# Order of rows and number of stores in the last token block of a fused retention + MLP kernel

## The chip, the cores and the metric

The kernel runs on one core of one Trainium2 chip. The metric is the device time of one execution in microseconds. Before the change it is 282.61 us, the median of 3 runs (282.43 to 282.74).

## The reference: what is computed

Inputs are q, k, v of shape (8 batches, 8 heads, 576 positions, 64) and two matrices, w_in (512 x 2048) and w_out (2048 x 512), all float32. The result is 4608 x 512, float32.

```python
scores = scale * np.matmul(q, k.transpose(0, 1, 3, 2))        # scale = 1/8
Dmat = np.where(rel >= 0, gamma[:, None, None] ** rel, 0.0)    # rel = i - j, one gamma for each head
attn = np.matmul(scores * Dmat, v)                             # retention: causal decay, no softmax
x = attn.transpose(0, 2, 1, 3).reshape(B * S, H * D)           # 4608 tokens x 512
h = x @ w_in
g = 0.5 * h * (1.0 + erf(h / sqrt(2)))                         # exact GELU
out = g @ w_out
```

## The kernel before

**Blocks and units.** The 4608 tokens are taken in 9 blocks (t = 0 to 8) of 512. A block is made of four units, ts = 0 to 3, each of them 128 token rows. Most units are 128 positions running of one batch. As 576 is 4 x 128 + 64, the ninth unit of each pair of batches is a short one: 64 positions of one batch and 64 of the next. `rows_of` (L1080) gives one range of output rows for an ordinary unit and two ranges of 64 rows for a short one. In the last block, t = 8, the units are 32 to 35 of 36, and ts = 3 is a short one.

**Second product.** For blocks 1 to 8, g times w_out is done with seven products of quarter size in place of eight (a Strassen scheme). The 512 tokens are split into an upper half (`half` 0: ts = 0, 1) and a lower one (`half` 1: ts = 2, 3), and the 512 output columns into two times 256. So there are four quadrants, named in the code c11 and c12 (upper half, left and right columns) and c21 and c22 (lower half). Within a half, r = 0 or 1 says which of its two units of 128 rows: a quadrant of one r is 128 rows x 256 columns, 128 KB. In the last block r = 0 stands for ts = 0 and 2, and r = 1 for ts = 1 and 3; so c21 and c22 of r = 1 are the short unit.

The products run in the order `SECOND = "1267534"` (L200), each of them for both r and in two parts of 8 matmuls. `fast` (L1146) issues the matmuls. What is done with the results stands in `add_second` (L1252): products 1 and 2 are copied from PSUM by ScalarE (product 2 of r gives c11, L1233); products 6, 7, 5, 3 and 4 are combined by ScalarE copies (L1243) and VectorE additions (L1238, L1247). The last VectorE addition for c22 hangs on product 5, that for c12 on product 3, that for c21 on product 4. In blocks 1 to 7 both r go through one chain (`rows_at_once`, L1141); in the last block each r has a chain of its own, with instructions of 128 x 256.

**Stores.** `store` (L1296) issues the DMAs on SyncE's queue, one for each range of rows that `rows_of` gives. In the last block there are, for each r, three store operations (L1358 to L1363): the whole lower half unit (512 columns) once c21 and c22 are there, c11 once it is there, and c12 once it is there. An ordinary unit is one DMA and a short one is two DMAs of 64 rows each. So the last block has seven DMAs: c11 of r = 0, c11 of r = 1, c12 of r = 0, c12 of r = 1, the lower unit of r = 0 (256 KB), and the lower unit of r = 1 (two of 64 x 512, 128 KB each). They are issued in this order.

**What sets the order.** A planner (class `Plan`, L30, and the loop at L1584) simulates the engines with assumed durations and gives out one operation after another: on each engine it takes, of those that can start within a small slack, the one with the lowest due time. The due times of the second product come from `W` (L324), which walks the `stream` of pieces in order (L311 to L315). SyncE works through its operations one after another, and waits at each for what the DMA reads. Besides, the DMAs use eight semaphores in turn, so that a DMA also waits until the eighth one before it has landed. After the last instruction SyncE waits at the end of the program for the DMAs of all eight (these waits carry L1654), and then all engines meet at a barrier.

Of the kernel before, what the change touches and what calls it, by code (L numbers as in the profile page):

```python
# [29 lines left out]
class Plan:  # L30
# [9 lines left out]
    def add(self, name, engine, dur, deps, fn, due=0.0, lag=0.12, **more):  # L40
        assert name not in self.ops, name
        op = self.ops[name] = Op(name, engine, dur, deps, fn, due, lag, **more)
        for d in op.deps:
            if d.startswith("land"):
                self.users.setdefault(d, []).append(op)
            dep = self.ops.get(d)
            if dep is None or dep.end is None:
                op.waits += 1
                self.later.setdefault(d, []).append(op)
            else:  # L50
                op.ready = max(op.ready, dep.end + dep.lag)
        if not op.waits:
            self.released(op)
        return op
# [53 lines left out]
def kernel(  # L108
# [23 lines left out]
    N_BLK = n_tok // TOK  # L132
# [28 lines left out]
    def slot_of(i):  # L161
        return pair_with(i)[0]

    v_order = [i for i in range(N_U) if i not in kept]
    n = v_order.index(pair_of[1, 1][0])
# [34 lines left out]
    SECOND = "1267534"  # L200
# [20 lines left out]
    add = P.add  # L221
# [81 lines left out]
    stream = []  # L303
    for t in range(N_BLK):
        if t < 2:
            cuts = CUTS if t == 0 else (0, 256, 512)
            for lo, hi in zip(cuts, cuts[1:]):
                stream.append([("1", t, m, 2, lo, hi) for m in K_ORDER[::2]])
        else:
            stream.append([one for block in LAYOUT[t] for one in laid(t, block)])  # L310
        if t < FAST:  # L311
            stream.append([("2", t, ts, m, m + 2) for m in range(0, N_DF, 2) for ts in range(2)])
            stream.append([("2", t, ts, m, m + 4) for ts in range(2, 4) for m in range(0, N_DF, 4)])
        else:
            stream.append([("2", t, p, r, n, part) for n, p in enumerate(SECOND) for r in range(2) for part in range(2)])  # L315

    def piece_time(one):
        if one[0] == "u":
# [6 lines left out]
    W = {}  # L325
# [6 lines left out]
    for one, at in W.items():  # L332
        key = ("1" if one[0] == "u" else one[0], one[1])
# [6 lines left out]
    for nm, src, eng, tag in (("q", q, nc.sync, "t"), ("k", k, nc.scalar, "t"), ("v", v, nc.sync, "o0")):  # L340
        t = first[nm] = (o_pool if nm == "v" else f_pool).tile([128, H, D], FP32, tag=tag, name=f"{nm}32")
# [214 lines left out]
    st = {i: {} for i in range(N_U)}  # L556
# [318 lines left out]
    for i in range(N_U):  # L875
        bp, ci, j = units[i]
        n = group_of[i]
# [28 lines left out]
        n, short = slot_of(i), i in tails  # L906
# [21 lines left out]
    for i in v_order:  # L928
        due = need[group_of[i]] + 3.0 if i not in kept else need[group_of[pair_of[1, 1][0]]] - 2.0
        n = v_order.index(i)  # L930
# [11 lines left out]
    for bp, ci in order_of_states:  # L942
# [16 lines left out]
        n = pair[0]  # L959
# [120 lines left out]
    def rows_of(t, ts):  # L1080
        bp, ci, j = units[t * 4 + ts]
        if j is not None:
            return [((2 * bp + j) * S + ci * C, 0, C)]
        return [((2 * bp + jj) * S + ci * C, TAIL * jj, TAIL) for jj in range(2)]
# [56 lines left out]
    def rows_at_once(t):  # L1141
        return [(0, 1)] if t < N_BLK - 1 else [(0,), (1,)]
# [153 lines left out]
    def store(t, half, cols=slice(None), rows=(0, 1), ends=True):  # L1296
        for r in rows:
            for row, p0, n in rows_of(t, 2 * half + r):
                nc.sync.dma_start(out[row:row + n, cols], fold["o", t, half][p0:p0 + n, r, cols])
        send("hw", T["sp"] + 1.0, STORE if ends and cols == slice(None) else STORE / 4)  # L1300
        if ends:
            o_ring[half].give(T["sp"] + 4.0)
# [12 lines left out]
    for run in stream:  # L1315
        for one in run:
            nm = f"mlp{one}"
            if one[0] == "1":
                _, t, m0, n, lo, hi = one
                xs = [f"x{i}" for i in range((t * TOK + lo) // C, (t * TOK + hi - 1) // C + 1)]  # L1320
                add(nm, "pe", piece_time(one), [f"land wi{m0 // 2}", *xs], lambda one=one: mlp1(one), W[one], DRAIN, banks=1)
                add(f"gelu{one}", "act", 0.08 + n * (hi - lo) * 0.00084, [nm, "warm_act"], lambda one=one: gelu(one), W[one] + 0.5,
                    at=lambda t=t, m0=m0: 0.0 if (t, m0 % 8 // 4) in g_tiles or not t else g_ring[m0 % 8 // 4].at())
            elif one[0] == "u":
                _, t, kp, p = one
                key = f"c{('u', t, kp)}"
                deps = [f"x{i}" for i in range(4 * t, 4 * t + 4)]
                deps += [f"ui{kp}.{LEFT[p]}"] if p in LEFT else []
                deps += [f"xs{t}.{RIGHT[p]}"] if p in RIGHT else []
                deps += [key + BEHIND[p]] if p in BEHIND else []  # L1330
                add(nm, "pe", piece_time(one), deps, lambda one=one: unit(one), W[one], DRAIN, banks=int(p in "321"))
                if p == PRODUCTS[-1]:
                    add_chain(("u", t, kp), 2, {q_: [f"mlp{('u', t, kp, q_)}"] for q_ in PRODUCTS},
                              {q_: W["u", t, kp, q_] for q_ in PRODUCTS})
            elif isinstance(one[2], str):
                _, t, p, r, n, part = one
                kps = (2 * part, 2 * part + 1)
                rs = next(x for x in rows_at_once(t) if r in x)
                key = f"c{('2', t, rs)}"
                deps = []  # L1340
                if p in G_SUM:
                    deps += [f"gs{t},{part}.{G_SUM[p]}"]
                else:
                    deps += gelus_of(t, kps, int(p != "1"))
                deps += [f"ws{kp}.{W_SUM[p]}" for kp in kps] if p in W_SUM else []
                deps += [f"land wo{kp + 4 * (p != '1')}" for kp in kps] if p in "123" else []
                deps += [key + BEHIND2[p] + (str(r) if p == "2" else "")] if p in BEHIND2 else []
                add(nm, "pe", piece_time(one), deps, lambda one=one: fast(one), W[one], DRAIN,
                    banks=int(not part and (p == "1" or p in OPENS and r == rs[0])))
                if p == SECOND[-1] and r == rs[-1] and part:  # L1350
                    at_ = {q_: {x: W["2", t, q_, x, SECOND.index(q_), 1] for x in rs} for q_ in SECOND}
                    add_second(("2", t, rs), len(rs), {q_: [f"mlp{('2', t, q_, x, SECOND.index(q_), 1)}" for x in rs] for q_ in SECOND},
                               {q_: max(at_[q_].values()) for q_ in SECOND})
                    if t < N_BLK - 1:
                        add(f"st{t},1", "sp", 1.1, [key + "c21", key + "c22"], lambda t=t: store(t, 1), W[one])
                        add(f"st{t},0", "sp", 1.1, [key + "c12"] + [key + f"c11{x}" for x in rs], lambda t=t: store(t, 0), W[one] + 1)
                    else:
                        add(f"st{t},1.{r}", "sp", 0.5, [key + "c21", key + "c22"],  # L1358
                            lambda t=t, r=r: store(t, 1, slice(None), (r,), ends=False), W[one])
                        add(f"st{t},0a.{r}", "sp", 0.5, [key + f"c11{r}"],  # L1360
                            lambda t=t, r=r: store(t, 0, slice(0, 256), (r,), ends=False), W[one])
                        add(f"st{t},0.{r}", "sp", 0.5, [key + "c12"],
                            lambda t=t, r=r: store(t, 0, slice(256, 512), (r,), ends=False), W[one] + 1)  # L1363
            else:
                _, t, ts, n0, n1 = one
                ms = K_ORDER[n0:n1]
                gl = [o for o in W if o[0] == "1" and o[1] == t and any(o[2] <= m < o[2] + o[3] for m in ms)
                      and o[4] < ts * 128 + 128 and o[5] > ts * 128]
                before = [f"mlp{('2', t, ts, 2 * n0 - n1, n0)}"] if n0 else []
                add(nm, "pe", piece_time(one), [f"land wo{m // 2}" for m in ms] + [f"gelu{o}" for o in gl] + before,  # L1370
                    lambda one=one: plain(one), W[one], DRAIN, banks=int(n0 == 0))
                if n1 == N_DF:
                    add(f"po{t},{ts}", "act", 0.5, [nm], lambda t=t, ts=ts: plain_out(t, ts), W[one] + 0.5,
                        at=lambda t=t, ts=ts: 0.0 if ("o", t, ts // 2) in fold else o_ring[ts // 2].at())
                    if ts % 2:
                        add(f"st{t},{ts // 2}", "sp", 1.1, [f"po{t},{ts - 1}", f"po{t},{ts}"], lambda t=t, ts=ts: store(t, ts // 2), W[one] + 1)
# [149 lines left out]
    for _ in range(N_WARM):  # L1526
        b, t = bank([128, 512], FP32, "warm")
# [131 lines left out]
```

## Time and profile before

| | us |
|---|---|
| median of 3 runs | 282.61 (282.43 to 282.74) |
| profiled execution: its time | 282.72 |
| profiled execution: span, first to last instruction | 280.7 |
| first matmul of the second product of the last block | 263.7 |
| last VectorE instruction (c21 of r = 1), start | 276.12 |
| last DMA issued by SyncE, start | 277.09 |

The granted TensorE clock is 1.000 over the whole span. The span is what the profile covers; the execution's own time is 2.0 us longer. An instruction row of the timeline gives start and length in us, the engine (SPq is SyncE's DMA queue, DVE is VectorE, PE is TensorE, ACT is ScalarE), the source line, what it writes and reads, and in brackets how long the engine had been idle before it and what ended that. For DMAs the instruction's length is only the issue; "to landing" is counted from the start of the issue to the completion of the transfer.

### The profile page before, as it was taken

The page shows a single profiled execution, that of the slowest core. Times are in us where ns is not written, and L with a number is a line of the kernel's source. Part 1 is how long each engine was busy: PE and PEld are TensorE (multiplying, and loading weights), DVE is VectorE, ACT ScalarE, POOL GpSimd, SP SyncE. Part 2 cuts the span into 40 slices and gives each one's busy share as a digit, 9 for nine tenths or more (in the row PEclk, how much of TensorE's full clock was granted, in tenths as well). Part 3 has the DMA queues.
Part 4 walks back from the last instruction along what each step waited for, and adds up shares of the span by engine and source line. Part 5 has one row for each costly group of instructions (what it writes and reads, how often), then busy time and mean ns, then how long its engine had stood idle before and what let it go on. Part 6 is the DMA issues. An engine that isn't in the chain of part 4 may idle for free.

```text
span 280.7 us, 8896 instructions
## 1 busy us (share of the span) xinstructions
PE 273.9 (98%) x3731; PEld 220.0 (78%) x3731; DVE 230.1 (82%) x438; ACT 174.0 (62%) x414; POOL 110.4 (39%) x139
## 2 busy tenths in 40 slices
PE   7999999999999999999999999999999999999993
PEld 2679767578888688868887888688868888888782
DVE  5870465699999998999799999987987799969832
ACT  7678733646438952995297319852898379528740
POOL 8967778847546086233326804705000000000000
PEclk9999999999999999999999999999999999999999
DMA  9999999999999999999989999999800040022013
GB/s 148 165 182 186 178 186 165 142 238 133 127 139 173 197 114 128 140 230 145 156 188 57 134 112 172 210 117 135 184 22 2 6 149 2 4 75 77 0 40 112
DMA packets 152071, 35.57 MB, mean 127 GB/s; under 512 B 141024, under 2 KB 147680, under 8 KB 152032
## 3 DMA queue, kind: packets, MB, share of 16 engines
q0 software_dynamic: 115792, 17.97, 98.1%
q1 hardware_dynamic: 35200, 16.78, 34.9%
q8 instruction: 29, 0.48, 0.8%
q10 hardware_dynamic: 1040, 0.26, 0.4%
q14 instruction: 10, 0.08, 0.1%
HBM read 36.70 MB, written 9.44 MB: 164 GB/s over the span
## 4 chain that ended last, share of the span: by engine, by line
PE 87%; DVE 4%; POOL 4%; DMA 3%; issue 1%; ACT 0%; POOLq 0%; DVEq 0%
PE oT L229 39%; PE hT L229 16%; PE zT L229 10%; PE yT L229 7%; PE o_ps L229 4%; DMA w_in<-in_moe_w_in_dram 3%; PE sc L229 2%; POOL qk_ld L517 2%; PE u_ps L229 2%; DVE s L999 1%; PE qk_ps L233 1%; DVE ret L652 1%; POOL v_ld L517 1%; POOL w_in L523 1%; DVE g L999 0%
## 5 line engine op out<-in xcount | busy, mean ns | idle before, releaser
L229 PEld LDWEIGHTS <-g 128*128 128x128 bf16 x576 | 55.1, 98 | 12.5 <-issue 0.2
L229 PEld LDWEIGHTS <-w_in 128*128 128x128 bf16 x656 | 53.0, 98 | 13.3 <-DMA w_in<-in_moe_w_in_dram 0.4
L229 PE MATMUL hT<-xT,w_in 128*128 128x128 bf16 (+2 forms) x480 | 53.5, 266 | 0.3 <-DMA w_in<-in_moe_w_in_dram 0.3
L229 PEld LDWEIGHTS <-wi_sum 128*128 128x128 bf16 x440 | 42.8, 98 | 6.6
L1099 ACT ACTIVATE g<-hT 128x512 bf16<-128x512 f32 (+1 forms) x72 | 35.9, 505 | 19.5 <-PE hT L229 17.7
L229 PE MATMUL oT<-w_out,g 128*128 128x256 bf16 (+1 forms) x320 | 45.6, 294 | 0.0
L517 POOL DMA_DIRECT2D qk_ld<-in_q_dram x31 | 28.0, 905 | 35.1 <-DMA qkT<-qk_ld 22.8
L229 PEld LDWEIGHTS <-s 128*128 128x128 bf16 x384 | 36.8, 98 | 5.6 <-DVE s L999 0.5
L517 POOL DMA_DIRECT2D v_ld<-in_v_dram x31 | 28.1, 910 | 22.8 <-ACT vh L824 9.5
L229 PE MATMUL oT<-w_sum,s 128*128 128x256 bf16 x256 | 32.4, 273 | 0.2 <-ACT o_sb L1243 0.2
L824 ACT ACTIVATE vh<-v_ld,dv 128x64 bf16<-128x64 bf16 x112 | 31.2, 346 | 1.0 <-DMA v_ld<-in_v_dram 1.0
L229 PE MATMUL oT<-w_sum,g 128*128 128x256 bf16 x256 | 30.8, 273 | 0.0
L517 POOL DMA_DIRECT2D qk_ld<-in_k_dram x31 | 28.0, 903 | 5.5 <-DMA v_ld<-in_v_dram 5.2
L1243 ACT COPY o_sb<-oT 128x512 f32<-128x512 f32 (+1 forms) x27 | 14.5, 538 | 25.2 <-PE oT L229 13.3
L1212 ACT ACTIVATE g<-zT 128x512 bf16<-128x512 f32 x44 | 25.9, 614 | 0.1
L652 DVE TENSOR_TENSOR ret<-sc,msk 128x512 bf16<-128x512 f32 x36 | 23.2, 687 | 1.4 <-PE sc L229 1.4
L1247 DVE TENSOR_TENSOR o_sb<-o_sb,oT 128x512 f32<-128x512 f32 (+1 forms) x27 | 16.8, 629 | 8.8 <-PE oT L229 4.5
L570 ACT COPY q<-yT 128x512 f32<-128x512 f32 x18 | 10.3, 594 | 21.8 <-PE yT L229 21.8
L855 DVE TENSOR_TENSOR xT<-o_ps,dqT 128x512 bf16<-128x512 f32 x26 | 16.8, 686 | 3.3 <-PE o_ps L229 3.3
L821 DVE TENSOR_TENSOR vh<-v_ld,dv 128x512 bf16<-128x512 bf16 x22 | 15.0, 688 | 3.4 <-DMA v_ld<-in_v_dram 3.4
L1221 DVE TENSOR_TENSOR zT<-q,zT 128x512 f32<-128x512 f32 x22 | 15.3, 695 | 1.0 <-PE zT L229 0.6
L1191 DVE TENSOR_TENSOR q<-q,zT 128x512 f32<-128x512 f32 x22 | 14.5, 684 | 1.7 <-PE zT L229 0.8
(170 smaller groups left out, 453.6 us busy)
## 6 DMA issues: line engine op xcount, KB each, us to landing
out_dram<-o_sb SPq DMA_DIRECT2D x30, 256.0 KB, 3.9
qk_ld<-in_q_dram POOLq DMA_DIRECT2D x31, 128.0 KB, 7.6
qk_ld<-in_k_dram POOLq DMA_DIRECT2D x31, 128.0 KB, 8.5
v_ld<-in_v_dram POOLq DMA_DIRECT2D x31, 128.0 KB, 8.0
w_in<-in_moe_w_in_dram POOLq DMA_DIRECT2D x8, 256.0 KB, 8.6
w_out<-in_moe_w_out_dram POOLq DMA_DIRECT2D x8, 256.0 KB, 7.8
out_dram<-o_sb SPq DMA_DIRECT2D x12, 128.0 KB, 2.7
v_ld<-in_v_dram POOLq DMA_DIRECT2D x8, 64.0 KB, 6.4
```

Source lines behind the costliest of these rows:

```text
L229: return nc.tensor.matmul(*args, **more)
L517: nc.gpsimd.dma_start(dst, src[2 * bp + j, :, ci * C:ci * C + C, :].rearrange("h s d -> s h d"))
L652: nc.vector.tensor_tensor(r, t, by, op=ALU.mult)
L821: nc.vector.tensor_tensor(vh, loaded[i][1], dv[:, :, ci:ci + 1].to_broadcast([128, H, D]), op=ALU.mult)
L824: nc.scalar.activation(vh[:, h], loaded[i][1][:, h], AF.Copy, scale=dv[:, h, ci:ci + 1])
L855: nc.vector.tensor_tensor(dst, o, dqT[:, :, ci * C:ci * C + C], op=ALU.mult)
L1099: nc.scalar.activation(g_of(t, m0)[:, m0 % 2:m0 % 2 + n, m0 // 8, lo:hi], hT, AF.Gelu)
L1191: nc.vector.tensor_tensor(q_, q_, chain[key]["Z"][1], op=ALU.subtract)
L1212: nc.scalar.activation(target(key, what), chain[key][n][1], AF.Gelu)
L1221: nc.vector.tensor_tensor(to, chain[key]["q"], z, op=ALU.add)
L1243: nc.scalar.copy(target(key, what), chain[key][n][1])
L1247: nc.vector.tensor_tensor(to, to, chain[key][n][1], op=ALU.add)
```

## The change

In the last block the two r change places: within each product r = 1 goes first, then r = 0. And the three store operations of each r become four, one for each quadrant: c11, c22, c12, c21, each waiting only for its own last instruction. Lower quadrants of r = 1 (the short unit) are two DMAs of 64 x 256 (64 KB each), all the others one of 128 x 256 (128 KB). That makes ten DMAs in place of seven, for the same 1 MB.

```diff
         else:
-            stream.append([("2", t, p, r, n, part) for n, p in enumerate(SECOND) for r in range(2) for part in range(2)])
+            stream.append([("2", t, p, r, n, part) for n, p in enumerate(SECOND) for r in ((0, 1), (1, 0))[t == N_BLK - 1]
+                           for part in range(2)])
...
                     else:
-                        add(f"st{t},1.{r}", "sp", 0.5, [key + "c21", key + "c22"],
-                            lambda t=t, r=r: store(t, 1, slice(None), (r,), ends=False), W[one])
-                        add(f"st{t},0a.{r}", "sp", 0.5, [key + f"c11{r}"],
-                            lambda t=t, r=r: store(t, 0, slice(0, 256), (r,), ends=False), W[one])
-                        add(f"st{t},0.{r}", "sp", 0.5, [key + "c12"],
-                            lambda t=t, r=r: store(t, 0, slice(256, 512), (r,), ends=False), W[one] + 1)
+                        for h, c, on in ((0, 0, f"c11{r}"), (1, 1, "c22"), (0, 1, "c12"), (1, 0, "c21")):
+                            add(f"st{t},{h}{c}.{r}", "sp", 0.4, [key + on],
+                                lambda t=t, r=r, h=h, c=c: store(t, h, slice(256 * c, 256 * c + 256), (r,), ends=False), W[one] + c)
```

## The prediction

> **What bounds the kernel now.** I read the page first, then the chain of waits, then the last 10 us of the timeline, engine by engine, then SyncE's stores one at a time and its waits at the end.
>
> ```profile
> span 280.7 us, 8896 instructions
> PE 273.9 (98%) x3731; PEld 220.0 (78%) x3731; DVE 230.1 (82%) x438; ACT 174.0 (62%) x414; POOL 110.4 (39%) x139
> ...
> PE 87%; DVE 4%; POOL 4%; DMA 3%; issue 1%; ACT 0%; POOLq 0%; DVEq 0%
> ```
>
> TensorE is busy for 98% of the span: nearly all of the time is matmuls. The change touches none, so what it can move is the stretch behind the last one. In the timeline of VectorE:
>
> ```profile
> 273.03 0.89 DVE L1247 TENSOR_TENSOR o_sb<-o_sb,oT 128x256 f32<-128x256 f32 x2 [0.45 <-ACT o_sb L1243]
> 274.37 0.42 DVE L1247 TENSOR_TENSOR o_sb<-o_sb,oT 128x256 f32<-128x256 f32 x1 [0.45 <-PE oT L229]
> 275.24 0.42 DVE L1247 TENSOR_TENSOR o_sb<-o_sb,oT 128x256 f32<-128x256 f32 x1 [0.45 <-PE oT L229]
> 276.12 0.42 DVE L1247 TENSOR_TENSOR o_sb<-o_sb,oT 128x256 f32<-128x256 f32 x1 [0.45 <-PE oT L229]
> ```
>
> Quadrants come out every 0.87 us, paced by TensorE (each row ends an idle time "<-PE"); the last, c21 of r = 1, is done at 276.12 + 0.42 = 276.54. From there to 280.7 there are 4.1 us with no engine computing. SyncE's DMAs one at a time (start in us behind the durations in ns; below each, its time to landing): c12 of r = 1, the 256 KB store of the lower unit of r = 0, and the two stores of the short unit:
>
> ```profile
> L1299 SPq DMA_DIRECT2D out_dram<-o_sb x1: 333/333/333, 274.8 to 274.8; - x1
> DMA to landing us min/median/max: 1.7/1.7/1.7
> ...
> L1299 SPq DMA_DIRECT2D out_dram<-o_sb x1: 332/332/332, 275.7 to 275.7; - x1
> DMA to landing us min/median/max: 2.0/2.0/2.0
> ...
> L1299 SPq DMA_DIRECT2D out_dram<-o_sb x1: 472/472/472, 276.6 to 276.6; - x1
> DMA to landing us min/median/max: 2.3/2.3/2.3
> ...
> L1299 SPq DMA_DIRECT2D out_dram<-o_sb x1: 587/587/587, 277.1 to 277.1; - x1
> DMA to landing us min/median/max: 2.4/2.4/2.4
> ```
>
> The timeline gives these starts as 274.82, 275.69, 276.56 and 277.09. SyncE stands ready each time: a store starts 0.02 to 0.03 us after its VectorE instruction ends. Only the fourth waits for the queue, for 0.53 us behind the third. It lands at 277.09 + 2.4 = 279.47 or so (two decimals from the wait that it ends, next). SyncE's waits at the end of the program:
>
> ```profile
> L1654 SPq EVENT_SEMAPHORE  x6: 28/28/28, 279.5 to 279.8; - x6
> ...
> L1654 SPq DRAIN  x3: 7/7/7, 279.9 to 280.2; - x3
> ```
>
> The first of six comes free at 279.48 (the last store has landed); five more follow at 0.06 us each, then the barrier, 0.8 us. So the end is: last VectorE instruction, 0.55 us until the last issue, 2.4 us to landing, 1.2 us of closing.
>
> **The change part by part.** The sum is made against this execution: span 280.67, time 282.72; the median of 282.61 lies 0.1 below, and I subtract from the median.
>
> *TensorE, VectorE, ScalarE, GpSimd: 0.* The change swaps which 128 rows go first. The built order of the changed kernel has the same instructions of the same shapes with the same waits on these four; only addresses differ. So quadrants still come out at 272.57 (c22), 273.45, 273.92 (c12), 274.79, 275.66 (c21) and 276.54, of r = 1 and r = 0 in turn. Both r of one product read the same g and wait for the same GELUs, so the swap makes neither wait longer. If that cover were gone, a matmul group late by one quadrant would cost 0.87.
>
> *SyncE: three DMAs more.* Its new order, from the built program: c11 of r = 1, of r = 0; c22 of r = 1 (two), of r = 0; c12 of r = 1, of r = 0; c21 of r = 1 (two), of r = 0. No DMA is held by the eight semaphores: the last reuses that of c11 of r = 0, issued some 9 us before.
>
> First, is SyncE late when the last quadrants come? A pair of 64-row stores took 0.472 + 0.587 plus gaps of 0.05 = 1.16; a 128-row store 0.33 alone and up to 0.58 straight behind such a pair (the store at 226.75). With the dearer figures: c22 pair 272.60 to 273.76, c22 of r = 0 to 274.39, c12 of r = 1 to at most 275.02, c12 of r = 0 to at most 275.65, just before 275.66. With 0.38 per 128-row store the queue has caught up by 274.8. So the c21 pair starts at 275.69 either way.
>
> Next, the last store. The c21 pair holds SyncE for 1.16 (until 276.85) if 64 x 256 issues like 64 x 512, or for 0.77 (276.46, no wait) if like 128 x 256. Half the bytes should press less on the second issue; the form with 64 rows is the nearer row. I take 276.80, between 276.57 and 276.87. Before: 277.09. Gain 0.29.
>
> Landing: a 128 x 256 store takes 1.7 with nothing close ahead of it (c12, twice). Of a 128-row store behind a 64-row pair there is one row with no loads about, the 256 KB store at 226.75: 2.4, against 2.0 for such a store at 275.69, 0.4 more. The new pair has half the bytes of that one. So 1.7 to 2.1; I take 1.8, nearer to the row of its own form. Landing at 278.60 in place of 279.47: gain 0.87 in all, issue included.
>
> Closing: the last DMA uses the sixth of the eight semaphores in place of the third, so two waits follow in place of five: 3 x 0.06 = 0.18. The other stores have landed by then. The barrier of 0.8 stays.
>
> Sum: 0.87 + 0.18 = 1.05. 282.61 - 1.05 = 281.6 us. With both unknowns at their good ends (276.57 + 1.7 = 278.27): gain 1.38, 281.2. At their bad ends (276.87 + 2.1 = 278.97): gain 0.68, 281.9.
>
> [...] Two 128 KB stores in place of one of 256 KB, and 64 KB ones in place of 128 KB. In the trace a store of 128 KB lands 1.7 after its issue and one of 256 KB 2.0, and two issued 0.53 apart landed 0.65 apart: what is fixed about a store overlaps with that of the next. [...]
>
> **The rivals.**
>
> A. *The last store lands no sooner.* Late in the kernel, where no loads are under way, the stores that directly follow a 64-row store (226.12, 226.75 and 277.09) all took 2.4 to land. If it's the place behind 64-row stores that costs, the last store lands at 276.87 + 2.4 = 279.27: gain 0.20 + 0.18 = 0.38, 282.2 us, no measurable change. For it: three rows of three. Against: two are themselves of 64 rows, the third has 256 KB, and each had twice the bytes just ahead of it. [...]
>
> B. *SyncE becomes the bound (slower).* Seven issues lie between 272.60 and the last one. It decides where they take on average more than 0.71 (gap included): 272.60 + 7 x 0.71 = 277.57, and with 2.1 to landing and the 0.18 we are where we were. At 0.83, like the store at 119.9 (783 ns plus a gap), the last issue is at 278.4, landing at 280.5: loss 1.03 - 0.18 = 0.85, 283.5 us. For it: 0.6 is common in a row of stores, and 1.599 was seen at 172.9. Against: those long ones stand where loads fill the DMA engines, whereas here nothing else runs, and issues took 0.33 to 0.59.
>
> C. *A late DMA engine (slower).* The c11 store at 266.95 took 3.4 to land, since an instruction fetch of 16 KB was on the DMA engines. If such a fetch fell on the last store, it would land at 276.80 + 3.4 = 280.2: loss 0.73 - 0.18 = 0.55, 283.2. Against it: in the view of the DMA queues behind 269 us no instruction fetch shows, and TensorE's instructions are the same; only SyncE has five more.
>
> **How the numbers follow.** Differences under 0.2% (0.57 us) can't be told from none here. The forecast, 281.2 to 281.9, has 0.78: each of its rows is from the same ten microseconds. A has 0.13, B 0.06, C 0.03. Of A, 0.02 goes to faster (an issue at 276.6) and 0.11 to same. So faster 0.80, same 0.11, slower 0.09. Predicted: 281.6. The range takes in the forecast's ends, with the 0.15 by which runs of the kernel scatter below, and A: 281.1 to 282.4. Outside lie B, C and a little of A and of the low end, under 0.2.
>
> **What would show it.** Right: VectorE's last instruction still starts at 276.1 or so; SyncE's last two issues are a 64-row store at about 276.2 to 276.3 and a 128-row one at about 276.8 with 1.7 to 2.1 to landing; two closing waits behind it; the span about 279.6. Wrong: the last issue at 277.1 or later (the pair costs SyncE more than it did), 2.4 to landing (A), stores starting later and later from 272.6 on (B), an instruction fetch behind 270 (C), or a c21 instruction of VectorE that starts later than 276.12 because its tile is being read by the c22 store, which the built order of waits doesn't show.

## The result, and the profile after

The changed kernel takes 281.86 us (median of 9 runs, 281.61 to 282.08), the kernel before 282.78 beside it (median of 9; the 282.61 of the prediction is the median of the first three of these). The ratio is 0.9966, interval 0.9957 to 0.9975: 0.34% faster. The profiled execution took 281.89, its span is 279.9.

The end of VectorE's timeline in the changed kernel (start and length in us): the last two instructions that finish a quadrant, c21 of r = 1 and c21 of r = 0.

```profile
275.28 0.42 DVE L1248 TENSOR_TENSOR o_sb<-o_sb,oT 128x256 f32<-128x256 f32 x1 [0.45 <-PE oT L229]
276.15 0.42 DVE L1248 TENSOR_TENSOR o_sb<-o_sb,oT 128x256 f32<-128x256 f32 x1 [0.45 <-PE oT L229]
```

They stand where they stood, 0.03 later. So all of the gain in these two traces lies behind 276.57. SyncE's stores there one at a time: c12 of r = 0, the two stores of c21 of r = 1 (64 x 256 each), and the last one, c21 of r = 0.

```profile
L1300 SPq DMA_DIRECT2D out_dram<-o_sb x1: 400/400/400, 275.0 to 275.0; - x1
DMA to landing us min/median/max: 1.8/1.8/1.8
...
L1300 SPq DMA_DIRECT2D out_dram<-o_sb x1: 472/472/472, 275.7 to 275.7; - x1
DMA to landing us min/median/max: 1.9/1.9/1.9
...
L1300 SPq DMA_DIRECT2D out_dram<-o_sb x1: 587/587/587, 276.2 to 276.2; - x1
DMA to landing us min/median/max: 2.0/2.0/2.0
...
L1300 SPq DMA_DIRECT2D out_dram<-o_sb x1: 535/535/535, 276.9 to 276.9; - x1
DMA to landing us min/median/max: 1.9/1.9/1.9
```

The last issue starts at 276.93, 0.36 after its data is there, since the pair holds the queue; it lands at 278.86. And SyncE's waits at the end of the program:

```profile
L1652 SPq EVENT_SEMAPHORE  x3: 28/28/28, 278.9 to 279.0; - x3
...
L1652 SPq DRAIN  x3: 7/7/7, 279.1 to 279.4; - x3
```

Three waits where there were six: the one that the last landing ends, and two behind it.

The following table sets all kernels of this study on the same footing, since the last VectorE instruction ends at somewhat different times in the profiled executions (276.39 to 276.91 us). All columns are from the traces, in us: from the end of the last VectorE instruction to the start of the last issue; the length of that issue; from its start to landing; from landing to the end of the span; and the sum of first, third and fourth, which is the tail.

| kernel | late | issue | to landing | closing | tail |
|---|---|---|---|---|---|
| before | 0.55 | 0.59 | 2.38 | 1.21 | 4.13 |
| changed | 0.36 | 0.54 | 1.93 | 1.02 | 3.31 |
| changed, again | 0.36 | 0.54 | 1.93 | 1.04 | 3.33 |
| swap alone | 0.36 | 0.54 | 2.44 | 1.21 | 4.00 |
| split alone | 0.55 | 0.59 | 2.04 | 1.04 | 3.63 |
| last unit in one store | 0.36 | 0.54 | 2.23 | 1.09 | 3.68 |
| c21 pair issued by ScalarE | 0.03 | 0.33 | 2.23 | 1.02 | 3.28 |
| product 4 of r = 1 first | 0.22 | 0.40 | 1.80 | 1.03 | 3.05 |
| ... last store in row halves | 0.74 | 0.59 | 2.04 | 0.98 | 3.76 |
| ... last store in column halves | 0.67 | 0.45 | 1.64 | 0.99 | 3.30 |
| ... c21 pair issued by ScalarE | 0.03 | 0.33 | 1.71 | 1.03 | 2.76 |
| ... and c11 stores cut | 0.03 | 0.33 | 1.69 | 0.92 | 2.64 |

From the kernel before to the changed one the tail shrinks by 0.82: 0.19 by the earlier issue, 0.45 by the faster landing and 0.18 at the closing waits. The medians of the runs differ by 0.92.

### The profile page after: what moved, and what is told of

Read it like the earlier page. It is cut to its first block, busy times and chain, and to the rows that moved or that the text cites. A ratio compares the mean times of both kernels' runs of the same rounds, so it can differ in the third digit from the quotient of the medians.

```text
span 279.9 us, 8901 instructions
## 1 busy us (share of the span) xinstructions
PE 273.6 (98%) x3731; PEld 219.9 (79%) x3731; DVE 230.0 (82%) x438; ACT 174.0 (62%) x414; POOL 110.4 (39%) x139
## 4 chain that ended last, share of the span: by engine, by line
PE 88%; DVE 4%; POOL 4%; DMA 3%; issue 1%; ACT 0%; POOLq 0%; DVEq 0%
PE oT L229 39%; PE hT L229 16%; PE zT L229 10%; PE yT L229 7%; PE o_ps L229 4%; DMA w_in<-in_moe_w_in_dram 3%; PE sc L229 2%; POOL qk_ld L518 2%; PE u_ps L229 2%; DVE s L1000 1%; PE qk_ps L233 1%; DVE ret L653 1%; POOL v_ld L518 1%; POOL w_in L524 1%; DVE g L1000 0%
```

## The experiments

Two theories stood at the start. Theory I: a store lands a fixed time after its issue has ended, and what stretches is SyncE's issue. Theory L, rival A of the prediction: what stands behind 64-row stores lands 2.4 us after its issue, whatever its size.

### The two parts apart

Only the swap, with the store operations as before (the edit is against the kernel before):

```diff
-            stream.append([("2", t, p, r, n, part) for n, p in enumerate(SECOND) for r in range(2) for part in range(2)])
+            stream.append([("2", t, p, r, n, part) for n, p in enumerate(SECOND) for r in ((0, 1), (1, 0))[t == N_BLK - 1]
+                           for part in range(2)])
```

> Only the swap: r = 1 goes first in the last block, the stores stay as before (seven; the lower unit of r in one go once c21 and c22 are there). The last store is then the 256 KB one of r = 0, behind two stores of 64 x 512. Theory I (a store lands a fixed time after the END of its issue: 1.36 us for 128 x 256, 1.68 for 128 x 512, 1.78 for 64 x 512, 1.46 for 64 x 256; what stretches is SyncE's issue, 0.33 alone and 0.54 straight behind a 64-row pair): last issue 276.93 to 277.47, landing 279.15, five closing waits behind it as before: 0.35 us faster than before. Theory L (what follows a 64-row store lands 2.4 us after the start of its issue, whatever its size): landing 279.33, 0.15 faster. In both: less than half of what the whole change gave (0.92).

Measured: 282.59 against 282.71, ratio 0.9994 (0.9985 to 1.0003): no measurable gain; the tail is 0.14 shorter. The last store:

```profile
L1300 SPq DMA_DIRECT2D out_dram<-o_sb x1: 535/535/535, 277.3 to 277.3; - x1
DMA to landing us min/median/max: 2.4/2.4/2.4
```

Its start, 0.36 behind its data, and its issue of 0.54 are as theory I has them, but the landing was 2.44 after the start, 1.90 after the end of the issue and not 1.68. Theory L names the number, but for one case only, as the next runs show.

Only the split, r = 0 first (this edit and all that follow are against the changed kernel, where nothing else is said):

```diff
-            stream.append([("2", t, p, r, n, part) for n, p in enumerate(SECOND) for r in ((0, 1), (1, 0))[t == N_BLK - 1]
-                           for part in range(2)])
+            stream.append([("2", t, p, r, n, part) for n, p in enumerate(SECOND) for r in range(2) for part in range(2)])
```

> Only the split: one store for each quadrant, r = 0 still first; the last two stores are the 64 x 256 ones of the short unit. Theory I: last issue starts at 277.09 as before, takes 0.59, lands 1.46 after its end: 279.13, two closing waits behind it in place of five: 0.34 + 0.18 = 0.52 us faster than before. Theory L: landing 277.09 + 2.4 = 279.49, 0.18 faster by the closing waits alone. If swap and split simply added up, this would be 0.92 less what the swap alone gives.

Measured: 282.10 against 282.71, ratio 0.9974 (0.9963 to 0.9986); the tail is 0.50 shorter, where theory I said 0.52 and L 0.18. The last store is one of 64 rows behind another, and lands 2.04 after its start:

```profile
L1299 SPq DMA_DIRECT2D out_dram<-o_sb x1: 587/587/587, 277.0 to 277.0; - x1
DMA to landing us min/median/max: 2.0/2.0/2.0
```

So L falls: the place behind a 64-row store does not make 2.4. And the issue takes 0.59 as it did with twice the bytes. The parts don't add up: 0.14 and 0.50 give 0.64 of 0.82. In the table, the swap issues the last store 0.19 earlier in either case; alone it gives 0.06 of that back at the landing, behind a pair with 256 KB, whereas together with the split, where the last store has few bytes itself and few ahead of it, the landing is 0.11 shorter.

Both, but the lower unit of r = 0 in one store of 128 x 512, which is then the last:

```diff
                         for h, c, on in ((0, 0, f"c11{r}"), (1, 1, "c22"), (0, 1, "c12"), (1, 0, "c21")):
+                            if r or on in ("c12", f"c11{r}"):
...
+                            elif on == "c21":
+                                add(f"st{t},{h}.{r}", "sp", 0.4, [key + "c21", key + "c22"],
+                                    lambda t=t, r=r, h=h: store(t, h, slice(None), (r,), ends=False), W[one] + c)
```

> The whole change, but the lower unit of r = 0 goes in one store of 128 x 512 at the very end, once its c21 is there; so the last store is 256 KB behind a pair of 64 x 256. Theory I: last issue 276.93, 0.54 long, landing 1.68 behind its end: 279.15; the last DMA has the fifth of the eight semaphores, three closing waits follow: 0.33 + 0.12 = 0.45 us faster than before, 0.35 slower than the changed kernel: that is what splitting the last unit is worth. Theory L: no slower than the changed kernel by more than 0.06, as bytes don't matter.

Measured: 282.06 against 282.71, ratio 0.9978 (0.9969 to 0.9988); the tail is 0.45 shorter than before, as theory I said, and 0.37 longer than with the changed kernel. The last store:

```profile
L1300 SPq DMA_DIRECT2D out_dram<-o_sb x1: 535/535/535, 276.8 to 276.8; - x1
DMA to landing us min/median/max: 2.2/2.2/2.2
```

It lands 1.69 after the end of its issue (2.23 after its start), the figure that a 256 KB store had before with nothing close ahead of it (2.01 less 0.33). So behind a pair of 64 x 256 the data doesn't wait, and what is added shows in the issue alone (0.54 for 0.33). Behind the pair of 64 x 512 of the swap alone it also waited for data: there the two stores of the pair landed 0.69 apart and the last one 0.70 behind the second, and from 277.19 to 279.29 there is no moment without store data on the DMA engines, whereas here there is a pause of 0.19 ahead of the pair's second store. In the kernel before, the window 277.70 to 278.80, where only 64-row stores moved, ran at 205 GB/s, and 276.70 to 277.30, with the 128-row store, at 321. So the 64-row stores moved their data at 0.64 of that rate; no run here shows why.

### Whose queue is it?

```diff
+                            q_, by = ("act", nc.scalar) if (r, on) == (1, "c21") else ("sp", nc.sync)
-                            add(f"st{t},{h}{c}.{r}", "sp", 0.4, [key + on],
-                                lambda t=t, r=r, h=h, c=c: store(t, h, slice(256 * c, 256 * c + 256), (r,), ends=False), W[one] + c)
+                            add(f"st{t},{h}{c}.{r}", q_, 0.4, [key + on],
+                                lambda t=t, r=r, h=h, c=c, by=by: store(t, h, slice(256 * c, 256 * c + 256), (r,), ends=False, by=by), W[one] + c)
```

`store` issues its DMAs on the engine given as `by`; the queue `act` is ScalarE's.

> The whole change, but the two 64 x 256 stores of c21 of r = 1 are issued by ScalarE, which has nothing left to do by then; SyncE is free when c21 of r = 0 is done. Theory I with the cost in SyncE's own queue: last issue at 276.60, 0.33 long, landing 278.29, against 278.86 in the profile of the changed kernel: 0.57 us less than the changed kernel, 1.4 to 1.5 less than before. If the two queues share what makes the issue slow: SyncE's last issue starts at 276.60 but is stretched to 0.54 or more, or it waits for ScalarE's pair: landing 278.5 to 278.86, 0 to 0.35 less than the changed kernel. Theory L (the place behind 64-row stores on the DMA engines costs, whoever issues them): landing 276.60 + 1.93 = 278.53 at best.

Measured: 281.78 against 282.71, ratio 0.9968 (0.9956 to 0.9981): no more than the changed kernel gives; the tail is 3.28 for 3.31. The rows of ScalarE's pair and SyncE's last store (first and last start behind the durations; below, the landing of all three):

```profile
L1300 ACTq DMA_DIRECT2D out_dram<-o_sb x2: 546/573/600, 275.8 to 276.4; - x2
L1300 SPq DMA_DIRECT2D out_dram<-o_sb x1: 332/332/332, 276.7 to 276.7; - x1
...
DMA to landing us min/median/max: 2.0/2.2/2.2
```

SyncE's issue is now short (0.33) and starts 0.03 behind its data, as theory I had it for a cost in SyncE's own queue. But the store lands 2.23 after it, at 278.88, where 278.29 was expected (278.34 with the 0.05 by which VectorE ends later in this trace). From the first issue of the pair to the last landing it is 3.10, and 3.13 in the changed kernel. So theory I is too narrow. My reading, an inference from these two sums, is that something which both queues share takes the stores one after another, and the pair of 64 rows fills it; on one queue one sees this as a longer issue (0.54 for 0.33), on two as a later landing (2.23 where 1.7 is the figure with nothing close ahead). The stretch isn't the bandwidth of the DMA engines: a store with nothing close ahead of it (c12 and the 256 KB store before) moves its first data 0.49 after its issue ends, which here would be 277.48; in the trace no DMA engine moves store data between 277.43 and 277.62, and the first data of the last store start at 277.93. This run agrees with a sharing, but doesn't show what is shared; SyncE's own issue of 0.33, as short as alone, holds no wait.

### Is it the 64 rows, and do they have to be there?

In a last block with another order, product 4 of r = 1 stands ahead of product 3. So the short unit's c21 comes two quadrants earlier, ahead of both c12 ones, and the last three quadrants have 128 rows each:

```diff
-            stream.append([("2", t, p, r, n, part) for n, p in enumerate(SECOND) for r in ((0, 1), (1, 0))[t == N_BLK - 1]
-                           for part in range(2)])
+            order_ = [(p, r) for p in SECOND for r in range(2)]
+            if t == N_BLK - 1:
+                order_ = [(p, r) for p in SECOND[:5] for r in (1, 0)] + [("4", 1), ("3", 1), ("3", 0), ("4", 0)]
+            stream.append([("2", t, p, r, SECOND.index(p), part) for p, r in order_ for part in range(2)])
```

> The whole change, and in the last block product 4 of r = 1 goes ahead of product 3, so that c21 of the short unit comes out two quadrants earlier; the last three quadrants are c12 of r = 1, c12 of r = 0 and c21 of r = 0, all 128 rows. Theory S (the pair of 64-row stores is what holds the last store up: three stores need 3.1 us from the pair's first issue to the last landing, on one queue or on two): with the pair two quadrants away, SyncE's last issue starts when c21 of r = 0 is done, 276.6, takes 0.33 to 0.40 and lands 1.4 after its end: 278.35 to 278.4, 0.45 to 0.5 us less than the changed kernel, 1.3 to 1.45 less than before. Theory D (any three stores in the last two steps cost this, whatever their rows, since the DMA engines or what feeds them are slow): no gain over the changed kernel beyond 0.15.

> The changed kernel as it is, to stand beside the reordered one on one chip: 0.8 to 1.0 us less than before. Its trace says whether 0.47, 0.59 and 0.54 for the issues of a 64-row pair and the store behind it repeat to 0.01 us (a fixed cost) or scatter (contention).

Measured on one chip: 281.52 reordered and 281.73 changed, against 282.61; ratios 0.9962 (0.9949 to 0.9974) and 0.9965 (0.9951 to 0.9978). The times don't tell the two apart, the traces do: tails of 3.05 and 3.33, 0.28 less, where theory S said 0.45 to 0.5 and D no more than 0.15. The last store of the reordered kernel:

```profile
L1302 SPq DMA_DIRECT2D out_dram<-o_sb x1: 402/402/402, 276.7 to 276.7; - x1
DMA to landing us min/median/max: 1.8/1.8/1.8
```

It still starts 0.22 late. SyncE's queue shows why, the eight stores from c22 of r = 1 on merged into one row:

```profile
272.57 4.56 SPq L1302 DMA_DIRECT2D out_dram<-o_sb  x8
```

8 stores in 4.56 us, 0.57 each. Such a merged row hides the gaps between its stores; one at a time they are 0.05 to 0.09 throughout, so SyncE never waits for data here: two pairs close together put it behind, and it hasn't caught up at the end. That is where theory S's forecast falls short. In the repeated changed kernel the issues of a pair and the store behind it took 0.472, 0.588, 0.536 and 0.472, 0.592, 0.536; in the first profile 0.472, 0.588, 0.536 and 0.472, 0.587, 0.535. They repeat within 5 ns, as fixed costs would, and don't scatter as contention would.

The last store (128 x 256) of the reordered kernel, cut into two: first by rows, then by columns. Each edit shows only the loop that takes the place of this one store; it stands in a function `store_halves`.

```diff
+        for n in range(2):
+            nc.sync.dma_start(out[row + 64 * n:row + 64 * n + 64, 256 * c:256 * c + 256],
+                              o[64 * n:64 * n + 64, r, 256 * c:256 * c + 256])
```

```diff
+        for n in range(2):
+            cols = slice(256 * c + 128 * n, 256 * c + 128 * n + 128)
+            nc.sync.dma_start(out[row:row + 128, cols], o[:, r, cols])
```

> The reordered kernel, but its very last store (c21 of r = 0, an ordinary unit) is cut into two stores of 64 rows x 256. Theory S (64 rows cost): the two issues take 0.47 and 0.59 as those of the short unit do, landing 1.46 behind the second: 276.6 + 0.47 + 0.05 + 0.59 + 1.46 = 279.17. Theory D (two DMAs in place of one cost, whatever their form): the same landing as with two column halves, in the next run.

> The reordered kernel, but its very last store is cut into two of 128 rows x 128 columns, the same bytes as the row halves. Theory S: issues of 0.33 and about 0.40, as for stores of 128 rows in a row; landing 1.4 behind the second: 276.6 + 0.33 + 0.05 + 0.40 + 1.4 = 278.8, some 0.4 before that of the row halves. Theory D: no difference to the row halves beyond 0.1.

Measured, in one execution of each, the profiled one: 282.38 and 281.97. The row halves, then the column halves:

```profile
L1311 SPq DMA_DIRECT2D out_dram<-o_sb x2: 472/530/587, 276.8 to 277.3; - x2
DMA to landing us min/median/max: 1.9/2.0/2.0
```

```profile
L1312 SPq DMA_DIRECT2D out_dram<-o_sb x2: 396/420/445, 276.9 to 277.4; - x2
DMA to landing us min/median/max: 1.6/1.6/1.6
```

An ordinary unit cut into row halves costs just what the short unit's pair costs, 0.472 and 0.587; cut into columns 0.396 and 0.445. From the last VectorE instruction to landing it is 2.77 and 2.31: 0.46 apart, as theory S said (0.4), where D said 0.1. With the store in one piece it is 2.02 (0.22 + 1.80). So both theories have a part: two stores in place of one cost 0.29 even with 128 rows each, and the form of 64 rows costs 0.46 on top. The halves also differ in the length of a row's piece, 1 KB against 512 bytes, which no run here takes apart from the number of rows. Between pieces of 2 KB and 1 KB the issue shows no difference: 0.472 and 0.587 for a pair of 64 rows in the kernel before and in the changed one, and 0.33 for the 128-row stores before, of 256 and of 128 KB.

### The reordered kernel with the pair on the other queue

The reordered kernel, with the short unit's c21 pair on ScalarE's queue (the edits of both experiments together):

> The reordered kernel (product 4 of r = 1 ahead of product 3), and the pair of c21 of the short unit is issued by ScalarE. Theory S (SyncE's issues, 0.47 + 0.59 for a pair and 0.54 behind it, form one row without a gap from 272.6 on, and what is left of the lateness is this row): with one pair less on SyncE it has caught up by 275.7; the last issue starts 0.05 behind the last VectorE instruction, takes 0.33, lands 1.36 behind its end: from the end of the last VectorE instruction to landing 1.75 against 2.02 in the reordered kernel, 0.27 us less than that, 1.2 to 1.3 less than before. Theory G (both queues are fed by one thing, as ScalarE's pair in the earlier run held SyncE's last store up by as much as on its own queue): the pair is over by 275.2, so the last store is free of it in either case; it differs only for c12 of r = 1, which should land 1.7 to 2.2 after its issue rather than 1.7.

Measured: 281.24 against 282.70, ratio 0.9943 (0.9931 to 0.9956): the lowest ratio of the study. Its interval lies just below that of the changed kernel (0.9957 to 0.9975), though each stands beside its own runs of the kernel before. The tail is 2.76, 0.28 less than the reordered kernel's, where S said 0.27. The last store, and c12 of r = 1, which follows ScalarE's pair:

```profile
L1302 SPq DMA_DIRECT2D out_dram<-o_sb x1: 333/333/333, 276.5 to 276.5; - x1
DMA to landing us min/median/max: 1.7/1.7/1.7
...
L1302 SPq DMA_DIRECT2D out_dram<-o_sb x1: 337/337/337, 274.7 to 274.7; - x1
DMA to landing us min/median/max: 2.2/2.2/2.2
```

The last store now has the cheapest form seen for a whole quadrant: no wait, 0.33, 1.7. The second row is theory G come true: a short issue and a late landing behind the other queue's pair, 0.5 more, but in a place where nobody waits for it.

The same with the two c11 stores cut into column halves (`store_halves` as above, for c11), so that the last DMA uses the eighth semaphore; the edit is against the kernel just described:

```diff
-                                lambda t=t, r=r, h=h, c=c, by=by: store(t, h, slice(256 * c, 256 * c + 256), (r,), ends=False, by=by), W[one] + c)
+                                lambda t=t, r=r, h=h, c=c, by=by: store_halves(t, h, c, r) if (h, c) == (0, 0) else store(t, h, slice(256 * c, 256 * c + 256), (r,), ends=False, by=by), W[one] + c)
```

> The same, and the two early stores of c11 are cut into two halves of columns each (128 x 128): twelve DMAs, so that the last one has the eighth of the eight semaphores and no closing wait follows its own. By the closing term (0.06 for each wait that follows) 0.12 us less than the run before; if the waits cost nothing, or the two more DMAs cost something, no gain. From the last landing to the end of the span: 1.35 - 0.12 less the two waits, so about 0.9 against 1.02 in the reordered kernel.

Measured: 281.17, ratio 0.9948 (0.9934 to 0.9961). The time doesn't tell this from the run before; in the trace the closing is 0.92 for 1.03, 0.10 less where two waits of 0.06 make 0.12, and the tail 2.64 for 2.76; the rest lies in the landing.

## Why the prediction was right

*TensorE to GpSimd: 0.* Right: VectorE's last instruction at 276.15 for 276.12.

*SyncE before the c21 pair.* Right: the issue of c12 of r = 0 ended at 275.36, the pair began at 275.73, 0.03 after its data.

*The last issue.* Forecast 276.80, between 276.57 and 276.87; measured 276.93, or 276.90 less the 0.03 of VectorE, in either case outside its bounds. This term was mis-sized. I argued that half the bytes press less on the second issue. They don't: 64 x 256 takes 0.47 and 0.59 like 64 x 512, and ordinary rows cut into halves do too. In these runs the issue goes by the form, and where SyncE waits for a semaphore between two stores the gap is 0.09, not 0.05. The gain of the term was 0.19 for 0.29.

*Landing.* Forecast 1.8 within 1.7 to 2.1; measured 1.93, a gain of 0.45 for 0.58. I put the surplus of 0.4 behind a pair down to the data ahead, and as that was halved, counted 0.1 of it. Of 1.93 the issue is 0.54, and 1.39 follow, about as much as for c12 before (1.69 less 0.33). So the surplus is the longer issue, and as fixed as the pair's. It isn't so for every pair: behind the pair of 64 x 512, in the swap alone, data ahead did cost 0.2.

*Closing.* Right: 0.18 forecast, 1.21 to 1.02 measured, three waits for six; cutting c11 took away the other two for 0.10.

*Sum.* 1.05 forecast; 0.82 in the traces, 0.92 between the medians. The time, 281.86, lies near the upper end of the forecast's own range (281.2 to 281.9), for two reasons: both terms missed the same way, and I subtracted from 282.61, where the nine runs of the kernel before have 282.78. The landing at 278.86 stayed ahead of the bad end, 278.97, only because the upper end of the landing term, 2.1, had room for an issue that came later than its own bound; that is luck in the size, not in the mechanism. Nor were all the rows from the same ten microseconds, as I wrote: the 0.58 and the 2.4 behind a pair came from the store at 226.75.

*The rivals.* A fell by the landing of 1.93 and by the split alone. B was nearer than I gave it credit for: from 272.63 to the last issue at 276.93, seven issues with their gaps took 4.29 us, 0.61 each (0.57 without the 0.28 that SyncE waited for c21 of r = 1), where 0.71 would have eaten the gain; and in the reordered kernel the row of issues is what is left of the lateness. C didn't occur in the tail; an instruction fetch did fall on the c11 stores in every kernel (see the end). *More and smaller stores.* Taking the last 256 KB apart, so that c22 goes ahead, gained 0.37 (a tail of 3.31 for 3.68). But it doesn't go on: with the last 128 KB taken apart too, as column halves of 64 KB, the landing came 0.29 later (2.31 behind the last VectorE instruction for 2.02).

## What to carry to other kernels

At the end of a kernel, look at the last stores one by one: how long after its data the last one is issued, how long the issue itself lasts, and how long the landing takes; between the kernels of this study they differ by 0.7, 0.25 and 0.8 us. Here it paid to put the stores of few rows well ahead of the last one (the short unit's c21 two quadrants earlier: a tail of 3.05 for 3.33), and to leave the last to a full 128 rows with few bytes (128 KB against 256: 3.31 for 3.68), in one piece (3.05 against 3.30 and 3.76 in halves); that needs the order of the computation, not only that of the stores. Moving an expensive store to another queue helped only where there was time between it and the last one (3.05 to 2.76; straight ahead of the last one 3.31 to 3.28), as a store behind the other queue's pair landed 0.5 later.

## What the runs showed that I had not expected

- A store of 64 rows takes SyncE 0.47 us to issue and a second right behind it 0.59, the same to 10 ns for 64 KB and 128 KB, in the last block of all profiles; the 128-row store right behind them takes 0.54, and 0.33 with nothing close ahead.
- A store on one queue is held up by a pair on the other: behind ScalarE's pair, SyncE's issue stayed short in both orders of products (0.332 and 0.337), but the landing went from 1.7 to 2.2. What holds it up wasn't told apart.
- The second of the c11 stores took 1.09 to issue in the changed kernel, against 0.33 before. With the split alone and with ScalarE's pair in the original order of products it was 0.33 too, in all the other kernels 0.98 to 1.49. SyncE's next store comes 2.8 us later or more, so it costs nothing. The traces point at an instruction fetch of 16 KB, which keeps one DMA engine for 0.96 to 1.61 us: all nine long issues end 0.37 to 0.39 after the fetch does, and there the fetch had begun at most 0.56 after the start of the first c11 store; in the three kernels with the short issue it began 0.65 or more after it.
